# A fused delta rule and SwiGLU kernel: gate and value products regrouped from 11 for 12 into 15 for 18, and a recurrence in six visits with two banks

## The chip, the cores and the metric

The kernel runs on one core of a Trainium2 chip. The metric is device time in microseconds of one execution, the median of several runs. The engines are TensorE (PE; its weight loads are listed apart as PEld), VectorE (DVE), ScalarE (ACT), GpSimd (POOL) and SyncE (SP), which here only issues DMAs. All run their own queues in order.

## What is computed

```python
k_n = k / (np.linalg.norm(k, axis=-1, keepdims=True) + 1e-06)
for t in range(S):                                   # S = 768
    y[:, :, t] = q_t @ state                         # per batch and head
    v_old = k_n_t @ state
    state = state + beta_t * outer(k_n_t, v_t - v_old)
x = y.transpose(0, 2, 1, 3).reshape(B * S, H * D)    # 3072 x 384
g = x @ w_gate;  val = x @ w_val                     # 384 x 1536 each
out = (g / (1 + np.exp(-g)) * val) @ w_out           # 1536 x 384
```

There are 4 batches, 8 heads, and a head dimension of 48. Everything is fp32.

## The kernel before

The sequence is cut into 12 chunks of 64 positions; with 4 batches a chunk has 256 tokens. For a chunk c, the recurrence is solved as a block: a triangular system of 64 by 64 per head (`invert`, two chunks at a time, called a pair) is inverted and finished by `join`; `advance(c)` then takes four visits, which are separated so that other products stand between them: (1) state times keys and state times queries, (2) u from the inverse, (3) the state update and the part of y from u, (4) the transposes of y into `x_ffn`, the input of the feed-forward part.

The feed-forward part of chunk c runs on TensorE between the visits of chunk c + 1. Chunks 0 and 1 are computed plainly (`gate_val`, `output`), 128x256 matmuls for gate and value and 128x384 for the output. From chunk 2 (`FAST`) on, `gate_val_fast` and `output_fast` use fast matrix products. A round covers four of the twelve column blocks of the hidden layer, by 11 block products where a plain product has 12; a block product is four 128x128 matmuls (`product4`). Three rounds make a chunk, that is 132 matmuls. The sums of weight blocks that the products need are made once on VectorE (`sum_of_w`), kept in DRAM (`kept`) and streamed in for every round; the sums of x blocks are made per chunk (`sums_of_x`, four). Accumulators are the four banks `ffn_banks`; a partial result goes from bank to bank by a ScalarE copy (L1212, L1252, L1255) and a VectorE addition (L1366). `output_fast` does the output with 7 block products for 8, 42 matmuls of 128x192.

The recurrence uses two pairs of PSUM banks, `px` and `py`; each visit with two sets of products puts one into each.

The order on every engine is the program's, written out by hand: `point(c)` issues one visit of chunk c or one step of preparation (`prep_step`: transposes, Gram products, joins), `fill(n)` issues some steps of the inversion, `finish(c)` issues what is left. `invert(g)` for g above 1 does its substitution on GpSimd (62 operations); for g = 1 it does it on VectorE, during the outputs of chunks 0 and 1. There, between `hold.clear()` and the first fast chunk, also the weight sums are made (`sums_of_w`), and the last visits of chunk 2 run.

A line that carries the meaning of a round:

```python
product4(p_w, summed_w(1, c), x_t[:, 0], True)
nc.scalar.copy(m5, p_w)
...
plus(p_y, p_y, m5)
product4(p_v, plain(0, f2), x[:, 0, tok[1]])
```

Of the kernel before, what the change touches and what calls it, by code (L numbers as in the profile page):

```python
# [13 lines left out]
C = 64  # L14
# [6 lines left out]
def kernel(  # L21
# [51 lines left out]

    def ps_pair(name, tag):

        return pairs_of_banks[tag]
# [122 lines left out]

    pieces = []  # L200
# [5 lines left out]
    for t in range(FT):  # L206
        pieces.append((wo_sb, moe_w_out, t, 0, DM))
    assert DFF == 1536 and KT == 3 and DM <= PIECE and 2 * HH * C == 4 * PIECE
# [37 lines left out]
    def stage(n, after=None, queue=nc.sync):  # L246
        _, src, t, f0, m = pieces[n]
        name, lo = place_of[n]
        if name not in places:
            if name == "p_sb":  # L250
                places[name] = words(p_places[0])
            else:
                places[name] = work.tile(
                    [128, 2 * PIECE], U32, name="staged", tag=name, bufs=1
                )
        place = places[name][:, lo : lo + 2 * m]
        staged[n] = place
        if after is not None:
            nc.gpsimd.tensor_copy(place[:, 0:1], staged[after][:, 0:1])
        queue.dma_start(  # L260
            out=place, in_=src[t * 128 : (t + 1) * 128, f0 : f0 + m].bitcast(U32)
        )
# [86 lines left out]
    ORDER = ((0, 0), (1, 1), (0, 1), (1, 0))  # L349

# [208 lines left out]
    def turn(out, in_):  # L559

        for i in range(0, R, R // 2):
            at = slice(i, i + R // 2)
            nc.vector.transpose(out[:, at], in_[:, at])  # L563
            yield 1.5

    z1s = {}
    WAIT, MORE = "wait", "more"
# [198 lines left out]
    def late_z(g, zb):  # L766

        nc.vector.transpose(
            ztp[g % ZB].rearrange("p c h i -> p i (c h)")[:, R:C],
# [7 lines left out]
    def join_late(g, c, tags):  # L777


        zt, a, d_t = ztp[g % ZB], a_sb[g], z_late[g]  # L780
# [34 lines left out]
    def invert(g):  # L815

        a_v = a_of[g].rearrange("p (m i) -> p i m", i=C)
        z_v = ztp[g % ZB].rearrange("p c h i -> p i (c h)")
# [13 lines left out]
        for _ in range({1: 2, 2: 3}.get(g, 4)):  # L832
            yield WAIT
# [8 lines left out]
        if g > 1:  # L842
            for _ in substitute(mb, zb, nc.gpsimd):
                pass
            for _ in range(11):
                yield WAIT
# [9 lines left out]
        zt = ztp[g % ZB].rearrange("p c (m e) i -> p c m e i", e=2)  # L856
# [8 lines left out]
        for s in range(2):  # L865
            hi = slice(64 * s, 64 * s + R)
            for c in range(2):
                z = ztp[g % ZB][hi, c]
                nc.scalar.copy(z[:, :, 0:R], z[:, :, R:C])
                yield 1 if g == 2 else 2  # L870
# [6 lines left out]
    def join(g):  # L877

        zt, a, z1 = ztp[g % ZB], a_sb[g], z1s[g]
# [13 lines left out]
        nc.scalar.mul(t2, p_j, -1.0)  # L893
        yield
        p_j = ps_pair("p_j", "py").rearrange("p e (c m i) -> p e c m i", c=2, m=M)
        for c in range(2):
            for m in range(M):
                for e in range(2):
                    for s in range(2):
                        row, hi = QUADS[2 * s + e][0], QUADS[2 * s][0]  # L900
                        nc.tensor.matmul(p_j[hi, e, c, m], z1[row, c, m], t2[row, c, m])
        zt_v = zt.rearrange("p c (m e) i -> p e c m i", e=2)
        for s, copy in ((0, nc.scalar.copy), (1, nc.vector.tensor_copy)):
            hi = QUADS[2 * s][0]
            copy(
                zt_v[hi, :, :, :, R:C].rearrange("p e c m i -> p e (c m) i"),
                p_j[hi].rearrange("p e c m i -> p e (c m) i"),
            )
        spent.append(1.8)
        yield  # L910

    def advance(c):

        kn = kn_of(c)
        zt = ztp[c // 2 % ZB][:, c % 2]
# [205 lines left out]
    def w_s(n, c):  # L1121
        if n < 4:
            return units(hp[5 + n])
        return units(hp[10] if c == FAST else p_places[0][:, 0:512])

    def m5_of(c, r):
        early = c == FAST and r == 0
        return units(hp[13] if early else p_places[0][:, 512:1024])

    kept = {  # L1130
        (n, r): dram.tile([128, 4, 128], FP32, name=f"w_s{n}_{r}")
        for n in (1, 2, 4)
        for r in range(3)
    }
    x_t = const.tile([128, 3, 128], FP32, name="x_t")

    def w_pair(m, t, f):
# [4 lines left out]
    made_in = {  # L1142
        0: {1: hp[6], 2: hp[7], 4: hp[10]},
        1: {1: hp[1], 2: hp[2], 4: hp[0]},
        2: {1: hp[12], 2: hp[13], 4: hp[8]},
    }

    def sum_of_w(n, r):

        f1, f2 = 2 * r, 2 * r + 6  # L1150
        for m in range(2):
            s1, s2, s4 = (units(made_in[r][k])[:, 2 * m : 2 * m + 2] for k in (1, 2, 4))
            if n == 1:
                plus(s1, w_pair(m, 0, f2), w_pair(m, 1, f2))
            elif n == 2:
                minus(s2, s1, w_pair(m, 0, f1))
            elif n == 4:
                minus(s4, w_pair(m, 1, f1), s2)
            else:
                minus(w_pair(m, 0, f2), w_pair(m, 0, f1), w_pair(m, 0, f2))  # L1160
        if n != 3:
            nc.sync.dma_start(out=kept[n, r], in_=units(made_in[r][n]))

    sums_at = {
        2: [(1, 1), (2, 1), (4, 1)],
        4: [(1, 2), (2, 2), (4, 2)],
        6: [(3, 1), (3, 2)],
        8: [(1, 0), (2, 0)],
        12: [(4, 0), (3, 0)],
    }  # L1170

    def sums_of_w(f):
        for job in sums_at.pop(f, ()):
            sum_of_w(*job)

    def sums_of_x(c):

        left, right = slice(0, 128), slice(128, 256)
        b1, b2 = xts[c][:, 0], xts[c][:, 1]
        minus(x_t[:, 0], b1[:, right], b1[:, left])  # L1180
        minus(x_t[:, 1], b2[:, right], x_t[:, 0])
        minus(b1[:, right], b2[:, right], b1[:, right])
        minus(x_t[:, 2], b2[:, left], x_t[:, 1])

    summed = set()

    def x_sums(c):
        if c < NCH and c not in summed and steps("advance", c) >= 4:
            summed.add(c)
            sums_of_x(c)  # L1190

    ROUNDS = 3

    p_x, p_w, p_y, p_v = (units(bank) for bank in ffn_banks)
    tok = slice(0, 128), slice(128, 256)

    def product4(p, w, moving, start=False):
        for u in range(4):
            nc.tensor.matmul(  # L1199
                p[:, u], w(u), moving, start=start and u == 0, stop=True,  # L1200
                skip_group_check=True,
            )

    def plain(t, f):
        return lambda u: w_pair(u // 2, t, f)[:, u % 2]

    def summed_w(n, c):
        return lambda u: w_s(n, c)[:, u]

    def begin(c, r):  # L1210
        product4(p_x, plain(0, 2 * r), xts[c][:, 0, tok[0]], True)
        nc.scalar.copy(p_y, p_x)  # L1212

    def clear(part):
        area = ffn_banks[2 + part][:, 0:DH]
        nc.scalar.copy(area, mask_q[:, 0:1].to_broadcast([128, DH]))

    def gate_val_fast(c, r, fill):

        f1, f2 = 2 * r, 2 * r + 6  # L1220
        x, m5 = xts[c], m5_of(c, r)

        def next_sums(n):
            to = c + (r == ROUNDS - 1)
            if to < NCH:
                nc.sync.dma_start(out=w_s(n, to), in_=kept[n, (r + 1) % ROUNDS])

        def silu(p, n):
            nc.scalar.activation(  # L1229
                sil[:, n].rearrange("p (i n) -> p i n", i=2), p[:, 0:2], ACTF.Silu  # L1230
            )

        def times(p, n, f, j):
            nc.vector.tensor_tensor(  # L1234
                out=h_of(c, f, j),
                in0=sil[:, n].rearrange("p (i n) -> p i n", i=2),
                in1=p[:, 2:4],
                op=ALU.mult,
            )

        more = 1.5 if (c, r) <= (FAST + 1, 0) else 0

        def combo_and_fill(n):
            if c == FAST:
# [561 lines left out]
```

## Time and profile before

| | us |
|---|---|
| median of 3 runs | 699.12 (698.62 to 701.1) |
| span of the profiled execution, first to last instruction | 694.7 |
| outputs of chunks 0 and 1 (130.08 to 174.25) | 44.17 |
| chunk 2 (174.25 to 226.38) | 52.13 |
| chunk 3 (226.38 to 280.69) | 54.31 |
| chunk 8 (494.81 to 548.22) | 53.41 |
| chunk 11, first product to the end (647.36 to 694.7) | 47.34 |
| substitution of one inversion on GpSimd (pair 3, 260.9 to 299.5) | 38.6 |

The profile gives the span of its execution and no other time for it. Chunks are cut where the first matmuls of a chunk's first round start. In groups, names stand as output<-inputs with the count and the mean in nanoseconds; a matmul of fp32 counts as two instructions.

### The profile page before, as it was taken

To read this page: it belongs to the slowest core of one execution; us is meant where nothing else is said; L and a number is where in the kernel's file an instruction comes from. 1 tells how busy PE (TensorE), PEld (TensorE's weight loads), DVE (VectorE), ACT (ScalarE), POOL (GpSimd) and SP (SyncE) were. 2 spreads that over 40 slices of the span, in tenths; PEclk is the share of its full clock that TensorE was granted. 3 is DMA by queue.
4 is the path that set the end of the run, shared out by engine and by line. 5 is a ranking of instruction groups with operands and counts; after the bars stand their busy time and mean duration, and the time that the engine had idled before them with its cause. 6 is when DMAs were issued, how large, how long until landed. Compare 5 with 4: busy or idle time off the path is not lost.

```text
span 694.7 us, 25664 instructions
## 1 busy us (share of the span) xinstructions
PE 681.7 (98%) x11380; PEld 636.3 (92%) x11380; DVE 411.2 (59%) x856; ACT 259.5 (37%) x549; POOL 192.3 (28%) x310
## 2 busy tenths in 40 slices
PE   8899999999999999999999999999999999999997
PEld 4688888757999999999999999999999999999997
DVE  6886789798657755647446456455565345333342
ACT  4774876214442532344233244233143242142230
POOL 5010031106882128820038820328800000000000
PEclk9899999999999999999999999999999999999999
DMA  9578724017550621464423363233363221121210
GB/s 137 151 187 215 215 78 151 1 35 177 128 111 14 116 79 40 105 119 79 93 72 70 74 134 70 56 84 72 67 119 70 56 63 46 55 63 46 69 47 23
DMA packets 143854, 62.31 MB, mean 90 GB/s; under 512 B 122976, under 2 KB 126048, under 8 KB 143744
## 3 DMA queue, kind: packets, MB, share of 16 engines
q1 hardware_dynamic: 141536, 60.19, 37.1%
q8 instruction: 89, 1.46, 0.9%
q10 hardware_dynamic: 2080, 0.39, 0.4%
q0 software_dynamic: 128, 0.10, 0.1%
q14 instruction: 21, 0.17, 0.1%
HBM read 53.58 MB, written 7.08 MB: 87 GB/s over the span
## 4 chain that ended last, share of the span: by engine, by line
PE 96%; ACT 2%; issue 1%; DVE 1%; DVEq 0%; ACTq 0%
PE ffn L1199 43%; PE ffn L1405 20%; PE ffn L1295 9%; PE ffn L1322 4%; PE p_px L963 2%; PE p_px L924 2%; PE p_py L933 2%; PE p_px L1031 1%; PE p_py L521 1%; PE p_py L1019 1%; PE p_px L521 1%; PE p_py L1092 1%; PE ffn L983 1%; PE p_px L645 1%; PE p_px L983 1%
## 5 line engine op out<-in xcount | busy, mean ns | idle before, releaser
L1199 PE MATMUL ffn<-x_ffn,wg_sb 128*128 128x128 f32 x840 | 128.2, 275 | 0.2 <-ACT x_ffn L1098 0.2
L1199 PE MATMUL ffn<-x_ffn,wv_sb 128*128 128x128 f32 x840 | 128.1, 275 | 0.0
L1199 PEld LDWEIGHTS ffn<-x_ffn,wg_sb 128*128 128x128 f32 x840 | 111.1, 192 | 0.3 <-ACT x_ffn L1098 0.3
L1199 PEld LDWEIGHTS ffn<-x_ffn,wv_sb 128*128 128x128 f32 x840 | 110.7, 192 | 0.0
L1234 DVE TENSOR_TENSOR h_f<-sil,ffn 128x256 f32<-128x256 f32 x120 | 49.9, 417 | 78.2 <-ACT sil L1229 76.4
L1229 ACT ACTIVATE sil<-ffn 128x256 f32<-128x256 f32 x120 | 46.1, 384 | 132.5 <-PE ffn L1199 130.8
L1405 PE MATMUL ffn<-wo_sb,h_f 128*128 128x192 f32 x480 | 83.4, 327 | 0.0
L826 POOL TENSOR_TENSOR n_b<-mb,half 128x32 f32<-128x32 f32 x5 | 30.0, 6003 | 183.3 <-DVE mb L563 183.3
L1366 DVE TENSOR_TENSOR ffn<-ffn,p_sb 128x512 f32<-128x512 f32 x58 | 40.5, 698 | 64.1 <-ACT ffn L1255 62.8
L1405 PEld LDWEIGHTS ffn<-wo_sb,h_f 128*128 128x128 f32 x480 | 78.1, 190 | 0.4
L599 POOL TENSOR_TENSOR zb<-zb,tmp 128x31 f32<-128x31 f32 (+15 forms) x124 | 71.4, 576 | 9.7
L593 POOL TENSOR_TENSOR tmp<-zb,mb 128x31 f32<-128x31 f32 (+15 forms) x124 | 67.0, 541 | 16.0 <-DVE mb L580 6.6
L1199 PE MATMUL ffn<-x_t,h_f 128*128 128x128 f32 x480 | 61.0, 280 | 0.2 <-ACT ffn L1212 0.2
L1199 PEld LDWEIGHTS ffn<-x_t,h_f 128*128 128x128 f32 x480 | 56.2, 191 | 1.4 <-ACT ffn L1212 0.4
L1366 DVE TENSOR_TENSOR o_sb<-o_sb,ffn 128x192 f32<-128x192 f32 x49 | 17.2, 352 | 61.9 <-PE ffn L1405 60.7
L1212 ACT COPY ffn<-ffn 128x512 f32<-128x512 f32 x30 | 17.1, 571 | 63.9 <-PE ffn L1199 63.9
L1405 PE MATMUL ffn<-last_k,h_f 128*128 128x192 f32 x200 | 35.9, 327 | 0.0
L1363 DVE TENSOR_TENSOR h_f<-h_f,h_f 128x256 f32<-128x256 f32 x60 | 30.2, 512 | 9.2 <-PE ffn L1405 8.2
L1295 PE MATMUL ffn<-x_ffn,wg_sb 128*128 128x256 f32 x144 | 34.4, 385 | 0.0
L1295 PE MATMUL ffn<-x_ffn,wv_sb 128*128 128x256 f32 x144 | 33.8, 382 | 0.0
L1405 PEld LDWEIGHTS ffn<-last_k,h_f 128*128 128x128 f32 x200 | 32.9, 190 | 0.0
L1295 PEld LDWEIGHTS ffn<-x_ffn,wg_sb 128*128 128x128 f32 x144 | 26.5, 190 | 4.4 <-DVE wg_sb L309 0.8
(304 smaller groups left out, 1100.2 us busy)
## 6 DMA issues: line engine op xcount, KB each, us to landing
h_f<-w_s SPq DMA_DIRECT2D x60, 256.0 KB, 2.8
p_sb<-w_s SPq DMA_DIRECT2D x27, 256.0 KB, 2.6
vin<-in_v_dram SPq DMA_DIRECT2D x48, 96.0 KB, 3.1
out_dram<-o_sb SPq DMA_DIRECT2D x48, 96.0 KB, 2.2
kn<-in_k_dram SPq DMA_DIRECT2D x20, 192.0 KB, 4.5
zt<-in_moe_w_out_dram SPq DMA_DIRECT2D x6, 384.0 KB, 3.6
qpad<-in_q_dram SPq DMA_DIRECT2D x36, 64.0 KB, 3.3
w_s<-h_f SPq DMA_DIRECT2D x7, 256.0 KB, 4.0
```

Of the source, the lines that this page charges most:

```text
L593: engine.tensor_tensor(out=t_v, in0=zb[:, 0 : j + 1, j : j + 1].to_broadcast([128, j + 1, m]), in1=mb[:, j : j + 1, j + 1 : R].to_broadcas ...
L599: engine.tensor_tensor(out=zb[:, 0 : j + 1, j + 1 : R], in0=zb[:, 0 : j + 1, j + 1 : R], in1=t_v, op=ALU.add,)
L826: nc.gpsimd.tensor_tensor(out=n, in0=mb.rearrange("p j i -> p (j i)")[:, 0 : R * R : R + 1], in1=half, op=ALU.pow,)
L1199: nc.tensor.matmul(p[:, u], w(u), moving, start=start and u == 0, stop=True, skip_group_check=True,)
L1212: nc.scalar.copy(p_y, p_x)
L1229: nc.scalar.activation(sil[:, n].rearrange("p (i n) -> p i n", i=2), p[:, 0:2], ACTF.Silu)
L1234: nc.vector.tensor_tensor(out=h_of(c, f, j), in0=sil[:, n].rearrange("p (i n) -> p i n", i=2), in1=p[:, 2:4], op=ALU.mult,)
L1295: nc.tensor.matmul(ps[name][:, i], w_sb[:, t, (f + i) * 128 : (f + i + 1) * 128], xts[c][:, t], start=(t == 0 and i == 0), stop=(t == KT - 1),
L1322: nc.tensor.matmul(p_o, hs[c, f - f % 2][:, f % 2, bp * 128 : (bp + 1) * 128], wo_sb[:, f], start=(f == 0), stop=(f == FT - 1),)
L1363: nc.vector.tensor_tensor(out=out, in0=a, in1=b, op=ALU.subtract)
L1366: nc.vector.tensor_tensor(out=out, in0=a, in1=b, op=ALU.add)
L1405: nc.tensor.matmul(p[x, part], a(f - f % 2)[:, f % 2], b(f), start=not begun and f == 0, stop=f == FH - 1, skip_group_check=True,)
```

## The change

- A round now covers six column blocks and all three blocks of x's features, by 15 block products for 18 (`do_product`); two rounds make a chunk: 120 matmuls of 128x128. This holds for chunks 3 to 11 (`FAST = 3`). Chunk 2's gate and value are plain matmuls (`plain_product`), its output stays with 7 for 8.
- A round uses six accumulators ("registers") in six banks: the four `ffn_banks` and the two of `py`. Products accumulate into them; between, 6 copies (ScalarE) and 8 passes (VectorE) move sums from register to register (`do_copy`, `do_pass`).
- 13 sums of weights per round are made by GpSimd in the stage of the first outputs (`w_sums`); the ten that products use are written to DRAM. Four of them are then put in the place of plain weight blocks (`residents`); six per round are streamed through four places (`next_stream`), 12 loads of 256 KB a chunk.
- Ten sums of x blocks a chunk (`sum_of_x`).
- For chunks 4 to 11 the recurrence has six visits with only the banks `px` (`advance_narrow`): state by keys, u, state by queries, the part of y from u, the state update, the transposes. What reads a visit's banks is put off (`behind_visit`) and issued at the next point or at tokens e and g (`flush`). The Gram products of keys and queries become separate steps.
- The order within a chunk is written as strings of tokens (`STEPS`) that `chunk` reads: p/P a product of round 0/1, c/C a copy, a/A a pass, s/S and m/M silu and times, x y z w sums of h, k an output product, j a sum of x, v a visit, g a preparation step, f a fill.

```diff
+    W_SUMS = (
+        ("6", "w01", "w11", -1),
+        ("3", "6", "w02", -1),
...
+    )
+    PLAIN_W = {2: (1, 2), 4: (1, 1), 8: (1, 0), 9: (2, 2), 10: (2, 1)}
+    PLAIN_X = {2: (2, 0), 4: (1, 0), 8: (0, 0), 13: (0, 1), 14: (2, 1)}
+    RESIDENT = {0: (0, 0), 13: (0, 1), 3: (0, 2), 7: (2, 0)}
+    STREAM = (6, 1, 14, 12, 5, 11)
+    REGISTER = (3, 4, 2, 0, 2, 0, 3, 1, 2, 5, 5, 4, 5, 5, 3)
+    PASSES = (
+        (5, "r5", "c3", -1),
+        (4, "c2", "r5", 1),
+        (0, "r2", "c3", -1),
+        (1, "c4", "r0", -1),
+        (3, "c3", "r5", 1),
+        (4, "c4", "r5", -1),
+        (3, "r3", "c1", -1),
+        (3, "c5", "r3", -1),
+    )
+    COPIES = (3, 2, 3, 4, 1, 5)
...
+        p0 p13 c0 p8 p6 c1 p4 a0 a1 c2 v p10 a2 f p1 e p3 c3 a4 p9 f a3 f v
+        p14 e a5 p7 f f v c4 s1 a6 p2 e m1 p12 s2 f e p5 m2 c5 a7 v s5 s0 m5
+        p11 v s3 m0 s4 m3 m4 x0 y0 z0 P0 P13 C0 P8 P6 C1 f A0 P4 A1 C2 A2 P1 f
+        P10 P3 v C3 A4 A3 P9 f f P14 A5 P7 f e C4 S1 A6 v P2 M1 S2 e M2 P12 P5
+        C5 S5 S0 A7 M5 f v P11 x2 l1 k50 S3 M0 k20 S4 M3 l0 k10 M4 x1 k12 y1
+        y2 k30 z1 z2 k11 b1 e k21 e k22 L k40 k31 u2 g k32 u3 w0 k41 k52 g w1
+        k42 w2 k51 b4 L u5 F j0 j1 j2 f j3 j4 j5 j6 j7 j9 j8 k60 k61 k62 g u6
+        k71 k70 k72 e u7
...
+    def w_sums(n, places, engine):
+        for r, (name, a, b, sign) in w_jobs[:n]:
+            t = units(places[0])
+            places.append(places.pop(0))
...
+            for m in range(2):
+                engine.tensor_tensor(
+                    out=t[:, 2 * m : 2 * m + 2],
+                    in0=operand(a, m),
+                    in1=operand(b, m),
+                    op=ALU.add if sign > 0 else ALU.subtract,
+                )
+            made[name, r] = t
+            if name.isdigit():
+                nc.sync.dma_start(out=kept[int(name), r], in_=t)
...
+    def do_product(c, r, n):
+        key = c, r, REGISTER[n]
+        begun = key in registers
+        if not begun:
+            registers[key] = take(False)
+            written.add(registers[key])
...
+        for u in range(4):
+            nc.tensor.matmul(
+                p[:, u],
+                w[u],
+                moving,
+                start=not begun and u == 0,
...
+        if n in STREAM:
+            next_stream()
...
+    def do_copy(c, r, n):
+        of = COPIES[n]
+        place = copy_places[n % 2]
+        nc.scalar.copy(place, register(c, r, of))
+        used[of] = place
...
+    def do_pass(c, r, n):
+        d, a, b, sign = PASSES[n]
+        if (c, r, d) not in registers:
+            registers[c, r, d] = take(True)
...
+        (plus if sign > 0 else minus)(register(c, r, d), operand(a), operand(b))
...
+    def advance_narrow(c):
...
+        visit(crossed, lambda bp, j, par, b: kt[c][head_of(par), bp, j, b], of_state)
+        behind_visit(lambda: minus(r, r, p))
+        yield
...
+        behind_visit(lambda: nc.scalar.copy(uu, p))
...
+        yield
...
+        visit(crossed, lambda bp, j, par, b: qt[c][head_of(par), bp, j, b], of_state)
+        ends = p[:, :, :, 0 : NJ : NJ - 1, 0:1]
+        behind_visit(lambda: nc.scalar.copy(ends, ends))
+        yield
+        visit(crossed, lambda bp, j, par, b: pq[half_of(b), par, bp, j], of_u, False)
...
+        behind_visit(copies_of_y)
+        yield
+        if c < NCH - 1:
+            visit(
+                lambda bp, j, par, b: p[head_of(par), b, bp, j],
+                lambda bp, j, par, b: kn[half_of(b), bp, 2 * j + par, 0:D],
+                of_u,
+            )
...
-        for bp in range(NB):
-            point(2)
-            output(0, bp, fill, (4, 8))
-        output(1, 0, fill, (4, 8))
-        hold.clear()
-        first_blocks(True)
-        first_blocks(False)
-        point(2)
-        output(1, 1, fill, range(2, FT, 2))
-        finish(2)
-        x_sums(2)
-        sums_of_w(12)
-        for c in range(2, NCH):
...
-            for r in range(ROUNDS):
-                gate_val_fast(c, r, fill)
-            output_fast(c, fill)
-            finish(c + 1)
-            x_sums(c + 1)
+        first_outputs(STEPS[0], fill)
+        chunk(2, STEPS[1], fill)
+        whole_bank()
+        free_banks.extend((4, 5))
+        narrow.append(1)
+        for c in range(FAST, NCH):
+            chunk(c, STEPS[4 if c == NCH - 1 else 2 + c % 2], fill)
```

In the stage of the first outputs the matmuls of several output tiles alternate, and the 26 weight sums (`W` tokens) are spread between them; on GpSimd's own queue they stand behind the inversion of pair 1's first steps and before the substitution of pair 2, with the start of that inversion (its power) among them. `whole_bank` is one 128x512 matmul that writes a whole `py` bank once.

## The prediction

> **What bounds the kernel now.** I read the page's busy shares first, then the chain of waits in order of time, then windows by chunk, then groups by shape, then the timelines of VectorE and GpSimd around the stage that is rebuilt.
>
> ```profile
> PE 681.7 (98%) x11380; PEld 636.3 (92%) x11380; DVE 411.2 (59%) x856; ACT 259.5 (37%) x549; POOL 192.3 (28%) x310
> ```
>
> TensorE is busy 98% of the span. A busy PE need not be at its peak, so I price it by unbroken stretches in the chain of waits (start, length, instructions; an fp32 matmul is two instructions):
>
> ```profile
> 118.43 5.18 PE ffn L1295 x24
> ...
> 551.12 4.66 PE ffn L1199 x40
> 555.78 1.08 PE p_px L963 x64
> 556.86 5.56 PE ffn L1199 x48
> 562.41 0.86 PE p_px L1031 x64
> 563.28 0.93 PE p_py L1019 x64
> ...
> 612.99 1.08 PE p_py L1019 x64
> ...
> 647.36 29.57 PE ffn L1199 x264
> 676.93 13.67 PE ffn L1405 x84
> ```
>
> The last chunk has nothing in between: 29.57/132 = 0.224 us for a 128x128 matmul, 13.67/42 = 0.325 for 128x192. A plain 128x256 matmul (L1295) costs 5.18/12 = 0.432. Returning to the ffn products after an interruption costs 4.66 - 20 x 0.224 = 0.18 us, and a recurrence product standing alone costs 1.08 where right behind another it costs 0.93 (L1019 both ways).
>
> ```profile
> 548.22:598.79 50.57, 50.57 (x740) 49.86 (x740) 21.99 (x45) 13.84 (x30) 0.00 (x0) 1.00 0.21 57
> 598.79:647.36 48.57, 48.57 (x613) 48.05 (x612) 17.69 (x40) 13.83 (x30) 0.00 (x0) 1.00 0.20 58
> ```
>
> Windows cut at chunks 9 and 10 (length, then busy PE, weight loads, DVE, ACT, POOL, granted clock): PE fills them, at clock 1.00. Chunk 10 by prices: 29.57 + 13.67 + 1.08 + 0.93 + 1.08 + 1.08 + 0.89 for its visits + four returns of 0.18 = 49.0 against 48.57. From 226 us on PE waits for practically nothing; only work taken from PE, or a new wait of PE, moves the end.
>
> **The change, part by part.**
>
> *Products.* Chunks 3 to 11 issue 120 gate and value matmuls for 132: 9 x 12 x 0.224 = -24.2 us. Chunk 2 goes back to 72 plain matmuls: 72 x 0.432 = 31.1 for 29.6, +1.5. The output products stay at 42.
>
> *Visits.* For chunks 4 to 11 the state and query products no longer share a visit, nor do state update and output, and the two Gram products are separated too. Per host chunk (3 to 10) three products stand alone (3 x 0.15) and three more returns follow (3 x 0.18): 1.0 us, 8 times, +8.0. Nothing in the trace excludes that an entry overlaps the tail before it: +4 to +10.
>
> *One bank filled once* (a 128x512 matmul): 4 x 0.224 = +0.9. Four further interruptions in chunk 2: +0.7.
>
> *VectorE and ScalarE.* Ten more accumulator passes and three more copies per chunk, six more sums of x:
>
> ```profile
> L1366 DVE TENSOR_TENSOR ffn<-ffn,p_sb 128x512 f32<-128x512 f32 x58 | 40.5, 698 | 64.1 <-ACT ffn L1255 62.8
> L1252 ACT COPY p_sb<-ffn 128x512 f32<-128x512 f32 x29 | 17.0, 586 | 24.5 <-PE ffn L1199 24.2
> ```
>
> DVE: 10 x 0.70 + 6 x 0.28 = +8.7 us, on 28 to 33 us in the windows of chunks 3 to 8, so about 38 of 52. ACT +1.8 on about 18. Neither is full; what hides them is the products put between. I laid round 0 of an odd chunk by hand, 0.9 us a product, 0.15 for a semaphore: register 3 copied by 1.6 us, needed at 2.7; register 2 copied at 3.5, needed at 3.6; the pass into register 4 done at 4.3, needed at 5.7; register 1 at 9.3, needed at 11.4. Covers are 0.1 to 2 us. If the cover is gone a pass costs its 0.7, and a pass queued behind two transposes (L563, 1.2 each) costs up to 2.4, and the next product into that bank waits, then everything behind it on PE. Bounds per chunk: 0, or half the 6.7 us of long DVE operations that fall into rounds (mask, transposes, visit sums) = 3.4. I take 0.3, since the covers found are nearer none: 8 x 0.3 = +2.4.
>
> *DMAs.* Twelve 256 KB weight loads a chunk for nine; with 16 block loads, 2 of k, 4 of v and 4 stores 38 issues on SP at up to 0.7 us each, 26 of 52 us. A slot is asked for again four streamed products (about 10 us) later; eight block loads of 0.7 ahead of it plus 2.8 us to land are 8.8. Taken as nothing; gone, about 1 us a chunk.
>
> *Weight sums go to POOL, ahead of chunk 2.* 52 operations of 128x256 stand in POOL's queue before the inversion of pair 2, while VectorE still inverts pair 1. Before, VectorE made its sums itself after that inversion. Two timelines (start, length, engine) show what POOL and VectorE do to each other:
>
> ```profile
> 183.87 0.91 DVE L1390 TENSOR_TENSOR h_f<-h_f,h_f 128x256 f32<-128x256 f32 x1
> ...
> 188.89 1.38 DVE L1363 TENSOR_TENSOR last_h<-wo_sb 128x1152 f32<-128x1152 f32 x1
> ...
> 195.90 0.43 DVE L1390 TENSOR_TENSOR h_f<-h_f,h_f 128x256 f32<-128x256 f32 x1
> 196.36 0.76 DVE L1363 TENSOR_TENSOR h_f<-h_f,h_f 128x256 f32<-128x256 f32 x1
> ```
>
> ```profile
> 184.57 0.67 POOL L593 TENSOR_TENSOR tmp<-zb,mb 128x240 f32<-128x240 f32 x1
> ...
> 189.13 1.65 POOL L593 TENSOR_TENSOR tmp<-zb,mb 128x255 f32<-128x255 f32 x1
> ```
>
> A DVE sum of two SBUF tensors takes 0.42 alone and 0.43 to 0.91 beside POOL, on average about +0.35; POOL's 0.65 became 1.65 while a 1.38 DVE operation ran.
> The Trainium skill (SBUF — State Buffer, "SBUF: two separate sides") calls the port that they share an exclusive lock held for the whole instruction; the 1.65 agrees, the 0.43 less so.
>
> The order then: POOL starts at 122 us (its copy into zb there is on the timeline), does 14 operations at 0.75 to 133, and stops, since its next place waits for a DMA that stands on SP behind the first output store, which is issued only after 16 of the 48 output matmuls, at 130.1 + 16 x 0.645 + 0.5 = 141; stored and landed, POOL goes on at 146 and works without a pause to 170. VectorE's inversion of pair 1 ended at 151.3 before; it is 1.6 behind at 146, and its last 24 operations (6.7 us) then take 24 x 0.35 longer: 161. Its transpose (2.2) ends at 163.3. The join for chunk 2 is due on PE at 130.1 + 44 x 0.645 = 158.5: a wait of 4.8, and 1.8 more for the ScalarE copies of the second transpose. Then chunk 2's remaining visits run with only two matmuls to cover: 0.9 for the copy of u, 1.5 for y. Together 9.0, where the chain of waits before shows 4.6 between 168.7 and 174.25 (y, x and this line):
>
> ```profile
> 172.01 0.64 ACT d_o L785
> ```
>
> Net +4.4; bounds -4.6 (all hidden) to +10 (each of the 24 operations waiting out a whole POOL operation, 24 x 0.65). The inversion of pair 2 on POOL begins near 186, takes 38.6 to 41.9 as in its two measured runs and ends by 228; VectorE needs it near 231, so nothing, or 3 if chunk 2 comes earlier.
>
> *Sum.* -24.2 + 1.5 + 8.0 + 0.9 + 0.7 + 2.4 + 4.4 = -6.3 us: span 694.7 to 688.4. The page gives only the span of its execution; the median, 699.12, is 4.4 above it, which I leave unchanged: 692.8, say 693 us.
>
> **The rivals.**
>
> *All covers hold.* No wait in the outputs and none per chunk: 693 - 4.4 - 2.4 = 686. For it: PE had no waits after 226 us with a similar mesh of copies and passes; against: 38 busy us of VectorE in 52 leave little play.
>
> *Whole-operation blocking between POOL and VectorE.* 24 x 0.65 = 15.6 for 8.4, so the join starts 7.2 later: 700. For it the 1.65 row, against it the 0.43 row.
> By the Trainium skill's lock, taken as it stands, this is the one that should happen.
>
> *VectorE sets the pace (the other side).* In a round, passes queue in order behind masks, transposes and visit sums; each chain of copy, pass, product then reaches PE late. Priced at 2 us a chunk for the 0.3 taken: 8 x 1.7 = +13.6, 706. It turns the result slower than before from a mean of 0.3 + 6.3/8 = 1.1 us a chunk. For it: the cover of 0.1 for register 2 and 15.7 us of VectorE work in a 19 us round with its transposes; against: in chunk 2's window before VectorE had 34 of 52 us and PE was busy throughout, and most covers are over 1 us.
>
> That fewer products would not be issued is no rival: the built order has 1080 such matmuls for 1320, and 72 plain ones.
>
> **How the numbers follow.** Forecast 0.42 (own range 689 to 699), all covers 0.27, whole blocking 0.15, VectorE's pace 0.16. The range 683 to 703 leaves out the slow rival's upper part (about 0.13) and a little below. A measurement here can tell 0.5% from no change, 3.5 us. Faster than 695.6: 0.27 and 0.35 of the forecast's 0.42, 0.62. Within: 0.07 and 0.15, 0.22. Slower: 0.16.
>
> **What would show it.** Per chunk from 4 to 10, the start of one chunk's first product to the next's should be 1.7 us shorter than before; if it is 2 shorter, covers hold; if equal, VectorE's pace. Matmuls of 0.224 in the last chunk should end it 2.7 earlier. The first product of the late join should wait for VectorE's transpose of zb, with chunk 2 starting near 179 us; at 174 or less the contention is mis-sized. Chunk 3 should start near 239. The forecast fails if PE waits over 1 us a chunk, or if a DMA of weights is what products wait for.

## The result, and the profile after

The changed kernel takes 724.3 us (median of 4 runs, 719.1 to 726.1) where the kernel before takes 698.9 (median of 4, measured beside it): 1.034 times as long, 95% interval 1.029 to 1.039. Its profiled execution has a span of 722.2 us against 694.7. The page's first part:

```profile
PE 675.2 (93%) x11046; PEld 616.2 (85%) x11046; DVE 482.0 (67%) x960; ACT 264.5 (37%) x567; POOL 230.3 (32%) x362
```

TensorE is busy 6.5 us less than before, and yet the span is 27.5 us longer, so its idle time grew by 34 us. Cut at the first product of chunk 3, the loss has two places. That product starts at 253.39 us. Before, chunk 3 started at 226.38, but two Gram products of 2.03 us that now stand ahead of it stood behind; with them, the same point lay at 228.4: 25.0 us are lost ahead of it. The time from there to the end is the second window below, beside the one of before (columns: window, then its length and the busy time of PE, weight loads, DVE, ACT, POOL, then granted clock, DMA share, GB/s).

```profile
228.40:694.70 466.30, 461.51 (x7460) 453.66 (x7449) 235.20 (x456) 149.67 (x318) 121.09 (x195) 1.00 0.33 73
```

```profile
253.39:722.20 468.81, 449.91 (x7188) 434.30 (x7188) 302.76 (x597) 156.95 (x344) 121.78 (x195) 1.00 0.38 89
```

Busy time fell by 11.6 us here, but idle time (length less busy) rose from 4.8 to 18.9 us, so nothing is left of the fewer products. The two windows of chunks 9 and 10, which stood in the forecast for before:

```profile
575.13:624.98 49.85, 48.85 (x716) 47.61 (x716) 28.68 (x61) 15.44 (x34) 0.00 (x0) 1.00 0.26 73
624.98:673.53 48.55, 47.16 (x588) 45.78 (x588) 24.71 (x56) 15.27 (x34) 0.00 (x0) 1.00 0.27 75
```

They are 0.72 and 0.02 us shorter than before, not the 1.7 that I had forecast, and each has 1.0 to 1.4 us of idle PE where before had none.

**Ahead of chunk 3.** TensorE's timeline around the join of chunk 2 (start, length, engine, line, and in brackets the idle time ahead):

```profile
157.61 3.07 PE L1686 MATMUL ffn<-wo_sb,h_f 128*128 128x384 f32 x9
173.84 0.59 PE L821 MATMUL p_px<-zt,a_sb 32*32 32x32 f32 x27 [13.16 <-issue]
```

All output matmuls ahead of the join are done at 160.7 and TensorE then stands still for 13.2 us. The page names no releaser ("issue"); VectorE's timeline does, and GpSimd's beside it says why:

```profile
150.44 0.83 DVE L622 TENSOR_TENSOR tmp<-zb,mb 128x255 f32<-128x255 f32 x1
151.31 0.83 DVE L628 TENSOR_TENSOR zb<-zb,tmp 128x255 f32<-128x255 f32 x1
...
171.07 0.20 DVE L622 TENSOR_TENSOR tmp<-zb,mb 128x31 f32<-128x31 f32 x1
171.31 0.21 DVE L628 TENSOR_TENSOR zb<-zb,tmp 128x31 f32<-128x31 f32 x1
171.56 2.18 DVE L797 STREAM_TRANSPOSE zt<-zb 128x1024 f32<-128x1024 f32 x1
```

```profile
150.09 0.90 POOL L1384 TENSOR_TENSOR last_h<-wg_sb,p_sb 128x256 f32<-128x256 f32 x1
150.96 0.90 POOL L1384 TENSOR_TENSOR last_h<-wv_sb,p_sb 128x256 f32<-128x256 f32 x1
```

The join reads zt, which the transpose at 171.56 writes. In this stretch the inversion of pair 1 goes forward in steps of 0.87 us, the same steps as GpSimd's weight sums. The last two operations, after GpSimd has stopped, take 0.2 us; they are only 31 columns wide, but one of the same width beside GpSimd, at 133.36, took 0.65.

**From chunk 3 on.** The start of chunk 11, where no recurrence visit and no transpose competes: PE, then ScalarE, then VectorE.

```profile
674.25 0.61 PE L1461 MATMUL p_py<-zt,wg_sb 128*128 128x128 f32 x4
...
675.15 0.61 PE L1461 MATMUL p_py<-x_ffn,wg_sb 128*128 128x128 f32 x4
675.59 0.61 PE L1461 MATMUL p_py<-x_ffn,wv_sb 128*128 128x128 f32 x4
677.61 1.16 PE L1461 MATMUL p_py<-x_t,h_f 128*128 128x128 f32 x8 [1.41 <-DVE p_py L1741]
```

```profile
676.24 0.59 ACT L1478 COPY zt<-p_py 128x512 f32<-128x512 f32 x1 [6.91 <-PE p_py L1461]
```

```profile
676.86 0.70 DVE L1741 TENSOR_TENSOR p_py<-p_py,zt 128x512 f32<-128x512 f32 x1 [2.94 <-ACT zt L1478]
```

Product 0 (674.25) goes into register 3 and product 13 (675.15) into register 5; here both lie in p_py, in its two banks. The copy needs register 3 only, complete near 675.3. It starts at 676.24, when product 13 ends. Product 6 (677.61) adds to register 3 and needs only that the copy is through, at 676.83. It waits for the end of VectorE's pass, at 677.56, which writes register 5. Twice an operation waits for work on the other bank.

### The profile page after: what moved, and what is told of

It reads as the page before. It is cut to its first block, busy times and chain, and to the rows that moved or that the text cites. A ratio compares the mean times of both kernels' runs of the same rounds, so it can differ in the third digit from the quotient of the medians.

```text
span 722.2 us, 25373 instructions
## 1 busy us (share of the span) xinstructions
PE 675.2 (93%) x11046; PEld 616.2 (85%) x11046; DVE 482.0 (67%) x960; ACT 264.5 (37%) x567; POOL 230.3 (32%) x362
## 5 line engine op out<-in xcount | busy, mean ns | idle before, releaser
L1478 ACT COPY zt<-ffn 128x512 f32<-128x512 f32 x71 | 41.7, 587 | 103.0 <-PE ffn L1461 100.5
L1741 DVE TENSOR_TENSOR ffn<-ffn,zt 128x512 f32<-128x512 f32 x34 | 23.7, 698 | 28.0 <-ACT zt L1478 12.5
L1656 PE MATMUL ffn<-x_ffn,wv_sb 128*128 128x256 f32 x144 | 33.8, 382 | 0.0
L1496 ACT ACTIVATE sil<-ffn 128x256 f32<-128x256 f32 x72 | 27.6, 387 | 16.2 <-PE ffn L1461 9.1
L1461 PE MATMUL ffn<-zt,wg_sb 128*128 128x128 f32 x188 | 30.7, 286 | 1.1 <-DVE zt L1744 1.1
L1461 PE MATMUL ffn<-x_ffn,wg_sb 128*128 128x128 f32 x192 | 30.4, 281 | 0.0
L1686 PE MATMUL ffn<-wo_sb,h_f 128*128 128x384 f32 x88 | 30.3, 504 | 0.0
L1656 PEld LDWEIGHTS ffn<-x_ffn,wg_sb 128*128 128x128 f32 x144 | 26.5, 190 | 4.4 <-DVE wg_sb L329 0.8
L1656 PEld LDWEIGHTS ffn<-x_ffn,wv_sb 128*128 128x128 f32 x144 | 27.0, 190 | 3.7
L1544 PE MATMUL p_py<-wo_sb,h_f 128*128 128x192 f32 x144 | 28.1, 329 | 1.9 <-issue 1.8
L1461 PE MATMUL ffn<-x_ffn,wv_sb 128*128 128x128 f32 x192 | 29.3, 275 | 0.0
L1461 PE MATMUL ffn<-zt,wv_sb 128*128 128x128 f32 x188 | 28.7, 275 | 0.0
```

What stands on the lines that cost most here:

```text
L1461: nc.tensor.matmul(p[:, u], w[u], moving, start=not begun and u == 0, stop=True, skip_group_check=True,)
L1478: nc.scalar.copy(place, register(c, r, of))
L1496: nc.scalar.activation(sil_of(len(silus)), register(c, r, n)[:, 0:2], ACTF.Silu)
L1544: nc.tensor.matmul(area(x), a(f0)[:, f % 2], b(f), start=not begun and f == f0, stop=True, skip_group_check=True,)
L1656: nc.tensor.matmul(ps[name][:, i], w_sb[:, t, (f + i) * 128 : (f + i + 1) * 128], xts[c][:, t], start=(t == 0 and i == 0), stop=(t == KT - 1),
L1686: nc.tensor.matmul(all_banks[p_o[c, bp]][:, 0:DM], hs[c, 2 * pair][:, f % 2, bp * 128 : (bp + 1) * 128], wo_of(f), start=(f == 0), stop=(f ...
```

## The experiments

Two theories came out of this comparison. For the stage ahead of chunk 3: the two engines, both reading pairs of SBUF tensors, hold each other up; its rival, that the inversion is handed over late. For chunks 3 to 11: operations on the two banks of one tile are put in order with each other; its rival, the prediction's own, that VectorE sets the pace.

**Thin sums on GpSimd.**

```diff
-    out=t[:, 2 * m : 2 * m + 2],
-    in0=operand(a, m), in1=operand(b, m),
+    out=t[:, 2 * m : 2 * m + 2, 0:16],
+    in0=operand(a, m)[:, :, 0:16], in1=operand(b, m)[:, :, 0:16],
```

> The 52 weight sums on GpSimd work on 16 of 128 columns each (the other columns of every sum are left out, and two 128x512 memsets are added). Theory (the two engines hold each other up for whole operations when both read two SBUF tensors): VectorE's operations of the inversion of pair 1 go back from 0.83 to 0.30-0.42 us, it ends near 151-153 us instead of 171.5, TensorE's wait ahead of the join goes from 13.2 to under 2, the granted clock stays at 1.00 in the 30 us behind it, chunk 3 starts near 231-235 instead of 253.4; chunks 3 to 11 stay at 468.8 +- 3; the time is 702 to 707. Rival (the inversion is late for another reason, e.g. it is handed to VectorE too late in the program's order): the wait stays above 8 us and the time above 715. Rival on the clock (the half clock is not caused by the idle time): TensorE still shows 0.5 for some 17 us near 170-195, and the time is near 711.

Measured: 713.0 us, 1.019 (1.016 to 1.023) of before. VectorE's same operations: two of 255 columns while GpSimd still waits for a DMA (it starts again at 146.37), and two of 240 columns with GpSimd's thin ones beside them, one of which follows:

```profile
144.67 0.43 DVE L622 TENSOR_TENSOR tmp<-zb,mb 128x255 f32<-128x255 f32 x1
145.13 0.42 DVE L628 TENSOR_TENSOR zb<-zb,tmp 128x255 f32<-128x255 f32 x1
...
147.40 0.41 DVE L622 TENSOR_TENSOR tmp<-zb,mb 128x240 f32<-128x240 f32 x1
147.85 0.41 DVE L628 TENSOR_TENSOR zb<-zb,tmp 128x240 f32<-128x240 f32 x1
...
155.93 2.23 DVE L797 STREAM_TRANSPOSE zt<-zb 128x1024 f32<-128x1024 f32 x1
```

```profile
147.44 0.48 POOL L1386 TENSOR_TENSOR last_h<-last_h,wv_sb 128x32 f32<-128x32 f32 x1
```

So 0.41 beside thin operations where the changed kernel has 0.82 for 240 columns (155.62). The inversion ends at 155.9 instead of 171.5, the join starts at 160.16 with no wait ahead of it, and chunk 3 at 239.96 instead of 253.39. So some 13 us are the two engines' contention. The rest of the expectation missed: the inversion still ends 4.6 us later than before (it starts at 132.6, before at 124.3: so much of the lateness the rival explains), chunk 3 starts 5 to 9 us later than I had expected, and chunks 3 to 11 took 4.7 us more than in the changed kernel. The trace shows where: the waits are nearly the same, but TensorE is busy for 454.6 us instead of 449.9, because its granted clock is at one half for 3.4 us in each of chunks 3, 6 and 8 (from 253.2, 403.7 and 550.5), where the changed kernel keeps 1.00.

**Two tiles for py.**

```diff
+    pool_y.__exit__(None, None, None)
+    pool_z = ctx.enter_context(tc.tile_pool(name="pool_z", ...))
+    all_banks[4:] = [pool_z.tile([128, 512], FP32, name=f"p_z{x}", ...) for x in range(2)]
     whole_bank()
```

> The bank pair py is given back before chunk 3 and allocated again as two tiles of one bank each; same instructions in the same order. Theory (operations on the two banks of one tile are put in order with each other though they touch different banks: in chunk 11 the copy of product 0's register waits for the end of product 13, and product 6 waits for a pass into the other bank): chunks 3 to 11 go from 468.8 us to 455-462, the last chunk from 48.7 to 45-46.5, the time to 710-717. Rival (VectorE's pace: its passes queue behind masks, transposes and visit sums, so products wait whatever the tile): chunks 3 to 11 within 2 us of 468.8, time 722-726. The stage before chunk 3 stays as it was in both.

Measured: 709.2 us, 1.014 (1.012 to 1.017). From the first register copy of chunk 3 to the end: 454.4 us instead of 467.6, 13.2 less. The start of chunk 11 again, PE and then ScalarE:

```profile
665.76 0.61 PE L1462 MATMUL p_z<-zt,wg_sb 128*128 128x128 f32 x4
...
666.65 0.61 PE L1462 MATMUL p_z<-x_ffn,wg_sb 128*128 128x128 f32 x4
...
667.54 1.10 PE L1462 MATMUL p_z<-x_t,h_f 128*128 128x128 f32 x8
668.48 0.61 PE L1462 MATMUL ffn<-x_ffn,wg_sb 128*128 128x128 f32 x4
```

```profile
666.85 0.59 ACT L1479 COPY zt<-p_z 128x512 f32<-128x512 f32 x1 [6.01 <-PE p_z L1462]
```

The copy now starts while product 13 is still going on, and product 6 follows without a gap. Not an instruction was removed or moved: the page counts the same ones on every engine (11046, 960, 567 and 362). From chunk 3 on, the waits of gate and value products for VectorE and ScalarE add up to 10.1 us in the changed kernel and to 1.1 here. So the order between the two banks comes with the tile that they shared, the program treating one tile as one object, and it cost 13 us.

**Two tiles, and VectorE's passes thin** (16 of 128 columns in each of the eight passes of a round).

```diff
-    (plus if sign > 0 else minus)(register(c, r, d), operand(a), operand(b))
+    (plus if sign > 0 else minus)(register(c, r, d)[:, :, 0:16], operand(a)[:, :, 0:16], operand(b)[:, :, 0:16])
```

> As e2_two_tiles, and the eight accumulator passes of a round work on 16 of 128 columns (the rest of each pass is left out). If VectorE's pace sets the waits that e2 leaves, they go too: chunks 3 to 11 another 5 us or more shorter than in e2_two_tiles, at 452 or less. If the order between the banks was all of it, the two runs agree within 2 us.

Measured: 707.9 us, and 452.4 us from chunk 3's first copy, 2.0 less than with two tiles alone, although VectorE is busy 62 us less in chunks 3 to 11. VectorE's pace is worth 2 us at most, not 13: two of the runs below that have two tiles and whole passes also show 452.7 and 452.8 us, so that even the 2 us do not stand clear of what differs from run to run.

**Both repairs** (thin sums, two tiles).

> e1_pool_sums_thin and e2_two_tiles together (GpSimd's sums thin, py as two tiles). If the two losses are separate, the savings add: about 20 us ahead of chunk 3 and 7 to 14 behind it, 689 to 697 us, faster than the kernel before. If the waits in chunks 3 to 11 only move, 700 to 706.

Measured: 699.65 us (10 runs), 0.999 (0.997 to 1.002) of before. The two losses are separate, and without them the kernel comes out level with the one before, not ahead of it as expected: chunk 3 starts at 244.5, 16 us later than before. Part of that is a surprise, the granted clock. Windows of this run (length, PE, ..., clock) against the thin sums alone:

```profile
168.00:173.00 5.00, 5.00 (x192) 5.00 (x192) 0.95 (x1) 0.31 (x1) 3.29 (x12) 0.50 1.00 357
173.00:178.00 5.00, 3.51 (x140) 3.18 (x132) 2.11 (x4) 1.25 (x2) 0.00 (x0) 0.50 0.06 19
178.00:183.00 5.00, 3.95 (x11) 2.75 (x12) 2.15 (x6) 1.77 (x4) 2.30 (x8) 0.50 0.00 0
```

```profile
163.00:168.00 5.00, 3.43 (x22) 1.71 (x26) 0.00 (x0) 2.31 (x4) 5.00 (x4) 0.68 0.71 115
168.00:173.00 5.00, 3.87 (x244) 3.58 (x238) 0.95 (x1) 0.80 (x1) 2.52 (x9) 0.98 0.90 324
173.00:178.00 5.00, 2.54 (x89) 2.20 (x83) 3.36 (x9) 1.66 (x4) 0.25 (x1) 1.00 0.03 10
```

With the same instructions in this stage, one run has half clock for some 17 us behind the join and the other for 3. From the join to chunk 2's first product they take 22.0 and 18.7 us: about 14 us more of half clock, and 3.3 us more time.

**Filling the wait.** Is it the idle time that brings the half clock? The first try at this put its matmuls under a condition on a chunk number that this call never has, so none was issued:

> The changed kernel with 18 more 128x384 matmuls on TensorE (identity times a part of the output weights, 0.645 us each, 11.6 us, the result is overwritten) right ahead of the join of chunk 2, in the 13.2 us in which it waits. Theory (the idle time brings the half clock): the granted clock stays at 1.00 from 160 to 195 us, chunk 3 starts at 246-248 instead of 253.4, the time is 716 to 719. Rival (the small 32- to 64-wide matmuls of the join and of the state products let the clock fall by themselves): the clock still shows 0.5 for over 8 us behind the join and chunk 3 starts within 3 us of 253.4, time 721 to 726.

It is the changed kernel once more: 721.2 us, chunk 3 at 252.37, 12.96 us of wait. That is a measure of how far two profiles of one program differ (253.39 above), and the clock has a part in it. Four runs share the order of this stage and the wait of 13 us ahead of the join: two tiles with thin passes, this one, two tiles, and the changed kernel. Behind the start of the join they have 5.7, 6.4, 8.7 and 9.3 us of half clock, and from there to chunk 2's first product they take 16.6, 17.0, 17.8 and 18.4 us: each us of half clock goes with about half a us of time. The second try issued them:

```diff
+    for _ in range(18 if (g, c) == (1, 0) else 0):
+        nc.tensor.matmul(banks("p_j", tags[0])[0][:, 0:DM], ident, wo_sb[:, 0])
     p_j = banks("p_j", tags[0])[0][:, 0 : M * R].rearrange("p (m i) -> p m i", i=R)
```

> The changed kernel with 18 more 128x384 matmuls on TensorE (identity times a part of the output weights, 0.645 us each, 11.6 us, the result is overwritten) right ahead of the join of chunk 2, in the 13 us in which it waits. Theory (the idle time brings the half clock): the granted clock stays at 1.00 until the join, and at most 4 us of half clock follow it (e1_pool_sums_thin, with 1.8 us idle, showed 3 to 4); chunk 3 starts at 246-249 instead of 252.4-253.4, the time is 715 to 719. Rival (the small 32- to 64-wide matmuls of the join and of the state products let the clock fall and keep it low): the clock shows 0.5 for over 8 us behind the join, chunk 3 starts within 2 us of the changed kernel's, time 720 to 726.

Measured: 720.4 us, chunk 3 at 253.11. Windows of the changed kernel and of this one:

```profile
168.00:173.00 5.00, 0.00 (x0) 0.00 (x0) 4.76 (x8) 0.00 (x0) 2.96 (x5) 0.50 0.81 130
...
178.00:183.00 5.00, 4.82 (x74) 2.94 (x71) 0.00 (x0) 2.30 (x4) 5.00 (x1) 0.50 0.01 3
183.00:188.00 5.00, 3.87 (x243) 3.52 (x240) 1.09 (x2) 0.80 (x1) 5.00 (x9) 0.99 0.30 108
```

```profile
168.00:173.00 5.00, 4.50 (x14) 2.29 (x13) 4.76 (x8) 0.00 (x0) 3.38 (x5) 1.00 0.72 88
173.00:178.00 5.00, 2.74 (x158) 2.31 (x159) 4.92 (x5) 1.75 (x3) 0.80 (x1) 0.81 0.46 163
178.00:183.00 5.00, 5.00 (x102) 3.25 (x106) 0.00 (x0) 2.30 (x4) 5.00 (x1) 0.51 0.01 3
```

The filled wait keeps the clock at 1.00 until the join, but it falls all the same, at 176, among the small matmuls of the join, and stays at one half until 183, as in the changed kernel. My theory in this form fell: the clock falls without the long idle time too. Shorter gaps are left, 1.50, 0.31 and 0.48 us within the 3.6 us ahead of the fall, so this run doesn't tell whether gaps or small matmuls bring it. From the join to chunk 2 it takes 18.0 us, between the 17.0 and 18.4 of the two profiles of the changed kernel: nothing was gained.

**Putting the sums elsewhere.** Six more kernels with two tiles, in which most of the sums come behind the inversion of pair 1. The first wrote sums into buffers that still held chunk 1's hidden values, ahead of chunk 1's last output matmuls, so that these waited 28.5 us and read other data (the diff shows the new end of the token string of chunk 2's stage and the gate; W is a sum, B a pair of output matmuls, v a piece of the recurrence):

```diff
+        ... v B110 f2 v v f2 W0 ... W25 f v B111 f2 v B112 B113 v B114 v B115 v F Y11 f4
+    nc.gpsimd.tensor_copy(hp[12][:, 0:1], p_places[0][:, 0:1])
```

> Two tiles as in e2_two_tiles; the 52 weight sums on GpSimd, whole, start only when VectorE has ended the inversion of pair 1 and both its transposes (a one-column copy on GpSimd reads what the second one wrote), into eight other buffers; and the join and the state products of chunk 2 stand between the last five pairs of output matmuls instead of behind them. Theory (the sums cost only by where they lie): VectorE's operations take 0.30-0.42 us, the inversion ends at 150-155, the join starts near 157, GpSimd sums until 192 and inverts pair 2 until 232, TensorE waits under 4 us in all before chunk 2, the clock stays at 1.00; chunk 3 starts at 235-240, chunks 3 to 11 take 455 +- 3 us, the time is 690 to 696, faster than before. Rival (the late inversion of pair 2 holds up chunk 3's join, or the sums then hold up VectorE's work of chunk 2): a wait over 3 us between 200 and 270, time 699 to 706.

725.4 us; only its chunks 3 to 11 tell anything (452.7 us from the first copy). The second put all 26 sums behind the outputs:

```diff
+        ... v B110 f2 v B111 v f2 B112 f2 f2 B113 v v B114 f2 v F B115 Y11 W0 ... W25 f4
```

> As e5_sums_after_join_spread without the changed order: join and state products of chunk 2 stand behind 44 output matmuls as in the changed kernel. Theory: inversion of pair 1 ends at 150-155, no wait ahead of the join at 160, waits of 5 to 6 us in all behind it as in e1_pool_sums_thin, the clock at one half for 3 to 16 us; chunk 3 starts at 240-246, the time is 696 to 702. If GpSimd's later end matters, a wait over 3 us near 250 and 702 to 708.

718.2 us. The inversion ended at 156.8, later than expected, and the join started at 161.0 without a wait, as expected; but TensorE waited 13.6 us at 213, because a sum on VectorE could not write last_h, from which the last weight sum was still being stored (VectorE's waits, 190 to 215 us: total, times, longest):

```profile
DVE last_h L1743 <- DMA w_s<-last_h: 19.8, 1, 19.8
```

The third took four sums ahead and spread the join between output matmuls:

```diff
+        W0 W1 W2 W3 v f B000 ...
+        f2 v v f2 f B111 v B112 v B113 v B114 v B115 v F Y11 W4 ... W25 f2 f2 f4
```

> Two tiles as in e2_two_tiles; four of the 26 weight sums (8 GpSimd operations) come first, before VectorE begins the inversion of pair 1, the other 22 only after it and its two transposes; join and state products of chunk 2 between the last four pairs of output matmuls. Theory: VectorE's operations take 0.30-0.42 us, the inversion ends at 150-155, the join starts at 158-160 without a wait over 1 us; GpSimd sums until 186-188, so the loads of k behind the stores in SP's queue come in time for the transposes needed near 197, and the inversion of pair 2 ends near 228; the half clock is seen for at most 4 us; chunk 3 starts at 234-239, chunks 3 to 11 take 455 +- 3 us, the time is 689 to 696, faster than before by 0.5 to 1.4%. Rival (SP's queue still holds back the loads of k, or the sums hold up VectorE's work of chunk 2): a wait over 3 us between 190 and 260, time 698 to 706.

721.1 us. Chunk 2 started at 176.9, the earliest yet; then VectorE waited for a power of 32 columns that stood behind the sums in GpSimd's queue, and TensorE 18.3 us for what stood behind it on VectorE:

```profile
DVE n_b L864 <- POOL n_b L856: 25.8, 1, 25.8
```

The fourth kept clear of both:

```diff
-    later_places = [hp[n] for n in (13, 10, 8, 9, 11, 12, 6, 7)]
+    later_places = [hp[n] for n in (13, 10, 12) + (6, 7, 9, 10) * 5]
+        f2 v v f2 f W4 W5 W6 f2 f2 B111 v ... v F Y11 W7 ... W12 L W13 ... W25 f4
```

> Two tiles, the join and state products of chunk 2 between the last four pairs of output matmuls, four weight sums first and three right behind VectorE's second transpose, as in e8_sums_in_two_parts; but the power of pair 2 (6 us on GpSimd, which VectorE waits for at 176) now stands ahead of the other 19 sums, these keep off the buffer last_h that VectorE writes near 190 (e7_sums_after waited 13.6 us for it), and the load of v goes out between the stores. Theory (what is left of the loss ahead of chunk 3 is only where the sums stand): join at 158-160, chunk 2 from 176-178, no wait over 2 us between 180 and 236, GpSimd's sums end by 200 and the inversion of pair 2 by 243; chunk 3 starts at 236-240, chunks 3 to 11 take 455 to 459 us, the time is 691 to 698, faster than before or the same. Rival (the sums find another thing to hold up, or pair 2 comes late to the join near 250): a wait over 3 us, time 698 to 706.

714.2 us. No wait over 2 us from 160 to 230; then VectorE came to the transposes of pair 2 before GpSimd, which had started that inversion at 206 instead of 194 as in the changed kernel, was through with it, and TensorE waited 13.75 us:

```profile
247.21 1.19 DVE L589 STREAM_TRANSPOSE zt<-zb 128x512 f32<-128x512 f32 x1 [12.97 <-POOL zb L629]
```

The last two had the planner hand VectorE these transposes later (17 and 15 turns of waiting for 11):

```diff
-    for _ in range(11 if g == 2 else 10):
+    for _ in range(17 if g == 2 else 10):
```

> e11_sums_clear_of_all waited in one place: VectorE took up the transposes of pair 2's inverse at 234 and waited 13.0 us for GpSimd, which had begun that inversion only at 205 and ended at 246; TensorE then waited 13.75 us for a sum of outputs queued behind them on VectorE. Here VectorE's program takes these transposes up later, behind the first five accumulator passes of chunk 3 (17 turns of waiting in the planner instead of 11). Theory: the 13.75 us go, chunk 3 starts at 239-242, its join comes later but no product waits over 2 us for it, chunks 3 to 11 take 454 to 458 us, the time is 694 to 699: faster than before by up to 0.7% or the same. Rival (the late join of pair 2 pushes chunk 4's visits together at the end of chunk 3): chunk 3 takes over 56 us, time 699 to 706.

> The same with 15 turns of waiting: the transposes stand behind the first three passes of chunk 3, near 245, so VectorE may wait 1 to 2 us for GpSimd's end at 246 and the next passes with it; otherwise as e12_turn_later_17, within 3 us of it.

730.6 and 725.5 us. Chunk 3 started at 239.7 and 240.1, as expected. But chunk 3 then took 58 us and chunk 4 69 and 71, for 53 and 52: the turns used for pair 2 were missing for pair 3, which GpSimd began 30 and 26 us later than with two tiles alone, and VectorE stood before its transposes:

```profile
346.01 1.19 DVE L589 STREAM_TRANSPOSE zt<-zb 128x512 f32<-128x512 f32 x1 [18.26 <-POOL zb L629]
```

In each order the wait went to the next place that hung on the queue the sums had been moved past. Of the kernels that compute the whole output, the two tiles alone are the fastest changed one, 1.4% slower than before. No run joined an early chunk 3 (239.7) to undisturbed chunks 3 to 11 (455.5 from the first product in the run with two tiles); their sum, 695.2, would be level with the span of before, 694.7, not under it.

## Why the prediction was wrong

I forecast 693 us, faster; it is 724. The span was to be 688.4 and is 722.2, 33.8 more.

*Products and visits: right.* With two tiles TensorE's busy time in chunks 3 to 11 is 446.3 us against 461.5 before, -15.2 where the steps -24.2 and +8.0 give -16.2. Chunks 9 and 10, between first copies, take 49.2 and 47.25 us, 1.3 less than before each (forecast 1.7).

*Waits per chunk, taken as 0.3 us: the step that failed most.* I laid out a round by what each operation needs, and found covers of 0.1 to 2 us. The program also orders operations on the two banks of py against each other, which I didn't look for, and the covers were gone: 13.2 us. By data alone they hold: with two tiles product 6 of the round above follows without a gap. With two tiles TensorE's idle time in these chunks is 9.2 us against 4.8 before, +4.4 for the +2.4 taken. "VectorE sets the pace" had nearly this price (+13.6) and the sign, and the check I had set for it, a chunk period as long as before, came true. Its mechanism is refuted all the same: with two tiles VectorE does the same work, and the loss is gone.

*The contention of GpSimd and VectorE: right in kind, too small.* I took 10.0 us: a first delay of 1.6, then 24 operations at +0.35 (the 6.7 us named for them hold 20 in the timeline of before). With thin sums the inversion ends at 155.9, with whole ones at 171.5, so the contention is 15.6 us: a wide operation takes 0.41 more, and more of them lie beside the sums. The other part is that both queues began later than I had them, GpSimd's sums at 128.1 (forecast 122) and the inversion at 133.0 (before 124.3); even with thin sums it ends 4.6 us later than before. So it ended at 171.5, not 161, and the join waited 13.2 us instead of 4.8. Of the 8.7 us by which the inversion starts later, 2.0 are that the whole stage started later, 132.1 against 130.1. For the rest, two multiplications by silu stand ahead of it in VectorE's queue and wait 3.15 and 3.13 us for TensorE (125.93 and 132.40); I had not looked for them in the changed order of VectorE's work.
The Trainium skill (SBUF — State Buffer, "SBUF: two separate sides") would have VectorE fully blocked for the whole of GpSimd's operation. The traces agree only in part: alone an operation comes every 0.45 us on VectorE (255 columns, thin sums) and every 0.69 us on GpSimd (near 130), which makes 1.14 in turn; together a pair takes 0.87.

*Net +4.4 for the outputs stage: the subtraction was wrong.* I took off 4.6 us of waits that the chain of before shows. These lay on the chain, but not on TensorE:

```profile
158.00:166.00 8.00, 7.88 (x248) 5.68 (x242) 7.24 (x17) 2.87 (x5) 7.12 (x1) 1.00 0.61 78
166.00:174.00 8.00, 7.66 (x221) 5.75 (x219) 5.90 (x15) 4.89 (x10) 4.13 (x8) 1.00 0.88 296
```

In these windows of before TensorE is busy for 15.54 of 16 us: outputs stood between the pieces of the recurrence and covered the copies. So only 0.5 us was there to take off. And the wait for y that I counted once comes twice, 1.59 us at 190.3 and 1.57 at 235.3. These two would be 5.7 of the 6.9 us by which the way from the join to chunk 3 is longer than my sum (79.5 for 72.6). But half the clock for 9.3 us, which the sum doesn't have, is worth 4 to 5 us at the rate of the four runs above, so that something else on this way must have come out cheaper than I took it; how the 6.9 us divide stays open. The sum itself puts chunk 3 at 235.9; the "near 239" written among the checks did not follow from it.

*One bank filled, plain chunk 2, DMAs:* these hold, but for 0.6 us. From chunk 2's first product to the filling of the bank the seven profiles with the changed kernel's order of this stage show 59.6 us (60.0 in the one with both repairs). The filling takes 1.5 us to chunk 3's first product (251.86 to 253.39) for the 0.9 taken, 0.51 of them a wait for a sum of x on VectorE. No product waits for a weight DMA.

Together: 13.2 for the banks, 3.1 for the rest of chunks 3 to 11, 2.0 for the later stage, 8.4 for the join's wait, 6.9 behind it (the 0.6 and the wait for y included): 33.6 of the 33.8 us.

## What to carry to other kernels

When a kernel splits a tile among independent jobs, look in the trace whether an operation starts at the end of the one that it needs or of a later one on the tile's other part; giving each job a tile of its own moved no instruction and was worth 13 us of 722. A wait on the chain is time to be won only where the engine that sets the end is idle in it; read it off that engine's busy share of the same window. Work moved to another engine's queue has to be priced there with both engines running, and past everything that waits behind it: each of four orders of the same 52 sums ended in another wait of 13 us or more at a place that had none.

## What the runs showed of the hardware

The granted clock fell to one half after short gaps. In the run with thin sums TensorE stood still for 1.83 us within the small matmuls of the join, and the clock fell as these ended, at 164.8; in the run with the filled wait it fell at 176.1, behind gaps of 1.50, 0.31 and 0.48 us. Small matmuls are not needed for it: the three falls in chunks 3, 6 and 8 with thin sums came behind gaps of 1.84, 2.18 and 1.49 us, and the second gap lies between 128x192 and 128x128 matmuls. Nor is such a gap enough: at the same place the changed kernel waits as long and keeps 1.00. The first product of chunk 6, with thin sums and in the changed kernel:

```profile
403.79 1.22 PE L1463 MATMUL p_py<-zt,wg_sb 128*128 128x128 f32 x4 [2.18 <-DVE o_sb L1746]
```

```profile
416.01 0.71 PE L1461 MATMUL p_py<-zt,wg_sb 128*128 128x128 f32 x4 [2.14 <-DVE o_sb L1744]
```

The same matmuls take 1.22 us at half clock and 0.71 at full clock. In those three places the half clock lasted 3.4 us each time. With both repairs it lasted 17 us (166.7 to 183.9), although the profile shows TensorE busy without a pause from 165.6 to 173.3, first with 128x384 matmuls, from 167.9 on with the small ones of the state products. The kernel before sends the same small matmuls of the join between 128x384 ones, has no such gaps there and keeps 1.00.
The Trainium skill (TensorE: Matmul & The Clock Gate, "Part 1: The HAM clock gate") lets the clock fall after an idle window of about 3.4 us and rise after a busy one of the same length. The three rises after 3.4 us agree with it. The falls came without an idle stretch of that length, and with both repairs 6.6 us of busy time at half clock did not bring it back. What decides between a gap that lets the clock fall and one that doesn't stays open.
